# A decode attention kernel: keys and probabilities transposed in 32x32 blocks on VectorE instead of on TensorE, with 128-column block-diagonal queries and 512-column matmuls

## The chip, the cores and the metric

The kernel runs on one core of a Trainium2 chip. Times are device microseconds of that core. "Span" is the time from the first to the last instruction in a profiled execution; the device time is some 1.7 us longer (198.0 and 199.75 us for the profiled run of the kernel before). All runs quoted are in the fast state (within 1.5% of the fastest of the same kernel) but one, which is named where it counts. In what follows, SBUF is the on-chip memory that transfers fill, and PSUM the eight banks into which TensorE writes; VectorE and ScalarE read both.

## The reference, cut to what matters

Four sequences each decode one token. The result is a gate times windowed attention, plus one minus the gate times a small feed-forward network. Attention has 32 query heads on 8 key/value heads of width 128 and looks at the last 4096 positions of the cache.

```python
q = (x @ wq).reshape(B, Sq, Hq, Dh)               # B=4, Sq=1, D=512, Hq=32, Dh=128
k = k_cache[:, :, Sk - W:, :]                     # Hkv=8, W=4096; each serves 4 query heads
v = v_cache[:, :, Sk - W:, :]
p = softmax(einsum("bhqd,bhkd->bhqk", q, k) * Dh ** -0.5)
a = einsum("bhqk,bhkd->bhqd", p, v).reshape(B, Sq, Hq * Dh) @ wo
b = ((relu(x @ W_gate)) * (x @ W_up)) @ W_down
out = g * a + (1 - g) * b                         # g = sigmoid(sum(x * gate_w))
```

All of it is bf16. 81 MB are read from memory, 67 MB of them keys and values, each used once.

## The kernel before

The work is cut into eight **sets**: one sequence and four key/value heads each. A set is 4.19 MB of keys and 4.19 MB of values. Keys arrive with positions on partitions. Scores need the head's width on partitions, so keys must be transposed. Before, TensorE does this, two bf16 at a time as one fp32, and VectorE and ScalarE share the copies out of PSUM:

```python
def KT(s, g):                                     # TensorE: 4 transposes fill one bank, 16 such groups in a set
    for q in range(4):
        c = 4 * g + q
        tp(bk[:, 128 * q:128 * (q + 1)], kf[:, 128 * c:128 * (c + 1)], identf[:, :], ...)

def EKT(s, g):                                    # VectorE (10 of 16) or ScalarE (6 of 16): back over the keys
    E.op(lambda: v.tensor_copy(kt_dst(s, g), bankb[tr(key)]), ev=("E",) + key, waits=[key])

def SC(s, f):                                     # scores: four column groups of 32 side by side, mask last
    for e in range(3):
        for c in range(4):
            lhsT, rhs = (maskl, maskr) if e == 2 else (qblk[:, s, e, :], kt[:, ck:ck + 4, :, e])
            mm(bk[32 * c:32 * c + 32, :], lhsT, rhs, e == 0, e == 2, ..., pos=(0, 32 * c))

def PV(s):                                        # probabilities times values, four side by side
    for c in range(16):
        for q in range(4):
            mm(ob(s)[32 * q:32 * q + 32, :], pT[:, s % 2, c, 32 * q:32 * q + 32],
               slot("v", s)[:, 256 * ck:256 * ck + 256], c == 0, c == 15, ..., pos=(0, 32 * q))
```

Each set then goes: four score blocks (`SC`), each reduced on VectorE (`ESC`); the row maximum over all four, shared between partitions by a small matmul (`MAX`, `SW`, `ESW`), which gives the negated maximum `negmax`; the exponential on ScalarE (`EXP`); the transposes of the probabilities (`PT`, TensorE, with copies `EPT`); the row sums (`RS`); the values (`PV`), normalised (`NORM`) and folded (`OQ`). The values of set s-1 are computed within set s. TensorE's order is fixed in the program:

```python
for s in range(1, NSET):
    o += kt(s, 0) + [("PT", s - 1), ("RS", s - 1)] + kt(s, 1) + [("SC", s, 0)] + kt(s, 2) + [("SC", s, 1)]
    o += kt(s, 3) + [("SC", s, 2), ("PV", s - 1), ("SC", s, 3), ("SW", s), ("OQ", s - 1)]
```

Five 4 MB slots in SBUF take the transfers in turn. A slot is asked for again when its reader is done.

## Time and profile before

| | before |
|---|---|
| time, median of 4 runs | 199.74 us (199.66 to 199.81) |
| span of the profiled run | 198.0 us |
| DMA | in all slices but the first and the last two at 90% or more |
| busiest engine | TensorE, 74% of the span |
| first and last `negmax` ready | 34.0 and 170.6 us, 19.5 us apart on average |

In the page's rows of slices each digit is the busy share, in tenths, of a fortieth of the span. In a timeline, the columns are start, duration, engine, line, operation, output and inputs, count and, in brackets, how long the engine sat idle before and what ended that. Most of the lines themselves are in the prediction below. These two are the first and the last maximum, ready at 34.04 and 170.58 us:

```profile
33.89 0.15 DVE L564 TENSOR_SCALAR negmax<-hmax 128x1 f32<-128x1 f32 x1
...
170.43 0.15 DVE L564 TENSOR_SCALAR negmax<-hmax 128x1 f32<-128x1 f32 x1
```

### The profile page before, as it was taken

To read this page: it belongs to the slowest core of one execution; us is meant where nothing else is said; L and a number is where in the kernel's file an instruction comes from. 1 tells how busy PE (TensorE), PEld (TensorE's weight loads), DVE (VectorE), ACT (ScalarE), POOL (GpSimd) and SP (SyncE) were. 2 spreads that over 40 slices of the span, in tenths; PEclk is the share of its full clock that TensorE was granted. 3 is DMA by queue.
4 is the path that set the end of the run, shared out by engine and by line. 5 is a ranking of instruction groups with operands and counts; after the bars stand their busy time and mean duration, and the time that the engine had idled before them with its cause. 6 is when DMAs were issued, how large, how long until landed. Compare 5 with 4: busy or idle time off the path is not lost.

```text
span 198.0 us, 4187 instructions
## 1 busy us (share of the span) xinstructions
PE 147.5 (74%) x1856; PEld 116.4 (59%) x1856; DVE 105.3 (53%) x245; ACT 67.4 (34%) x70; POOL 13.2 (7%) x38
## 2 busy tenths in 40 slices
PE   0029865999199949982998399929993999297854
PEld 0029732977197729762976397629772978155531
DVE  3005766786358747862786268626863676431100
ACT  2005721453425343434353425342534253410000
POOL 7774000000000000000000000000000000000000
PEclk9999999699859987999699669975998599855589
DMA  5999999999999999999999999999999999999981
GB/s 212 424 425 424 425 427 437 443 447 419 420 437 437 427 430 424 427 437 434 430 437 420 420 419 450 427 425 443 420 430 427 423 407 440 448 399 412 414 333 39
DMA packets 3946, 81.28 MB, mean 410 GB/s; under 512 B 588, under 2 KB 600, under 8 KB 984
## 3 DMA queue, kind: packets, MB, share of 16 engines
q1 hardware_dynamic: 3920, 81.01, 95.9%
q8 instruction: 14, 0.23, 0.5%
q14 instruction: 4, 0.03, 0.0%
q10 hardware_dynamic: 8, 0.00, 0.0%
HBM read 81.01 MB, written 0.00 MB: 409 GB/s over the span
## 4 chain that ended last, share of the span: by engine, by line
DMA 65%; PE 23%; SPq 7%; DVE 3%; issue 1%
DMA slots<-in_A_k_cache_dram 49%; DMA slots<-in_A_wo_dram 17%; PE bank L331 16%; SPq L258 7%; PE bank L327 7%; DVE qblk L542 1%; DVE sc L552 0%; DVE pe L527 0%; DVE slots L520 0%; DVE osum L600 0%; DVE pe L529 0%; DVE xT L523 0%
## 5 line engine op out<-in xcount | busy, mean ns | idle before, releaser
L331 PE MATMUL bank<-identf,slots 128*128 128x128 f32 x512 | 75.5, 311 | 28.5 <-DMA slots<-in_A_k_cache_dram 28.5
L331 PEld LDWEIGHTS bank<-identf,slots 128*128 128x128 f32 x512 | 68.3, 164 | 35.7 <-DMA slots<-in_A_k_cache_dram 29.2
L520 DVE COPY slots<-bank 128x1024 bf16<-128x1024 bf16 x80 | 54.4, 690 | 50.6 <-PE bank L331 49.4
L613 ACT ACTIVATE slots<-bank 128x1024 bf16<-128x1024 bf16 x48 | 47.6, 1022 | 65.2 <-PE bank L331 65.2
L635 ACT ACTIVATE pe<-sc,negmax 128x2048 bf16<-128x2048 bf16 x8 | 16.0, 2001 | 37.8 <-DVE negmax L564 37.8
L552 DVE TENSOR_SCALAR_CACHE_REDUCE sc<-bank 128x512 bf16<-128x512 f32 x32 | 22.1, 692 | 3.5 <-PE bank L327 1.2
L327 PE MATMUL bank<-slots,qblk 128*32 128x512 bf16 x256 | 20.3, 392 | 1.4 <-DVE qblk L542 1.2
L327 PE MATMUL bank<-slots,pT 128*32 128x256 bf16 x512 | 17.0, 291 | 0.7 <-DMA slots<-in_A_v_cache_dram 0.7
L327 PEld LDWEIGHTS bank<-slots,pT 128*32 128x32 bf16 x512 | 14.2, 103 | 3.5 <-DMA slots<-in_A_v_cache_dram 0.8
L331 PE MATMUL bank<-identb,pe 128*128 128x128 bf16 x128 | 13.7, 291 | 2.2 <-ACT pe L635 2.2
L331 PEld LDWEIGHTS bank<-identb,pe 128*128 128x128 bf16 x128 | 12.9, 139 | 2.7 <-ACT pe L635 2.3
L570 DVE COPY pT<-bank 128x1024 bf16<-128x1024 bf16 x16 | 10.9, 690 | 4.6 <-PE bank L331 4.5
L327 PE MATMUL bank<-maskr,maskl 128*32 128x512 bf16 x128 | 12.5, 377 | 0.0
L578 DVE TENSOR_SCALAR osb<-bank,recip 128x256 bf16<-128x256 f32 x8 | 3.9, 484 | 12.0 <-PE bank L327 12.0
L327 PEld LDWEIGHTS bank<-rd,grpb 128*128 128x128 bf16 x8 | 0.8, 96 | 14.2 <-DVE rd L558 14.2
L327 PE MATMUL bank<-rd,grpb 128*128 128x8 bf16 x8 | 1.4, 180 | 10.1 <-DVE rd L558 10.1
L327 PEld LDWEIGHTS bank<-slots,qblk 128*32 128x32 bf16 x256 | 4.6, 95 | 6.2 <-issue 3.5
L327 PE MATMUL bank<-slots,oq 128*4 128x256 bf16 x64 | 4.5, 272 | 2.6 <-DMA slots<-in_A_wo_dram 1.9
L327 PEld LDWEIGHTS bank<-maskr,maskl 128*32 128x32 bf16 x128 | 3.3, 94 | 3.9
L327 PEld LDWEIGHTS bank<-slots,oq 128*4 128x4 bf16 x64 | 2.3, 83 | 5.0 <-DMA slots<-in_A_wo_dram 3.4
L327 PE MATMUL bank<-slots,xT 128*4 128x512 bf16 (+1 forms) x64 | 5.1, 476 | 0.0
L327 PE MATMUL bank<-osb,fold 128*64 128x32 bf16 x64 | 3.6, 189 | 0.7 <-DVE osb L578 0.7
(57 smaller groups left out, 57.7 us busy)
## 6 DMA issues: line engine op xcount, KB each, us to landing
slots<-in_A_k_cache_dram SPq DMA_DIRECT2D x8, 4096.0 KB, 42.5
slots<-in_A_v_cache_dram SPq DMA_DIRECT2D x8, 4096.0 KB, 33.7
slots<-in_A_wq_dram SPq DMA_DIRECT2D x1, 4096.0 KB, 21.2
slots<-in_A_wo_dram SPq DMA_DIRECT2D x3, 1024.0 KB, 39.6
slots<-in_B_W_gate_dram SPq DMA_DIRECT2D x1, 1792.0 KB, 37.5
slots<-in_B_W_up_dram SPq DMA_DIRECT2D x1, 1792.0 KB, 40.8
wdsb<-in_B_W_down_dram SPq DMA_DIRECT2D x1, 1792.0 KB, 35.4
slots<-in_A_wo_dram SPq DMA_DIRECT2D x1, 512.0 KB, 42.4
```

The source lines that it names most:

```text
L258: E.op(lambda: e.dma_start(dst, src), ev=ev, waits=waits, ctr=ctr)
L327: E.op(lambda: t.matmul(out_, lhsT, rhs, start=start, stop=stop, tile_position=pos, skip_group_check=True), ev=ev, waits=waits)
L331: E.op(lambda: t.transpose(out_, in_, idn), ev=ev, waits=waits)
L520: E.op(lambda: v.tensor_copy(kt_dst(s, g), bankb[tr(key)]), ev=("E",) + key, waits=[key])
L542: E.op(lambda dst=dst, r=r, b=b: v.tensor_copy(dst, src[r, :, :, :, b]), ev=("E",) + key if (u, b) == (1, 3) else None, waits=[key, ("QZ",)])
L552: E.op(lambda: v.tensor_scalar(sc[:, 512 * f:512 * f + 512], banks[scb(key)], 1.0, None, op0=ALU.mult, op1=ALU.max, accum_out=mx4[:, f:f + ...
L570: E.op(lambda: v.tensor_copy(dst, bankb[tr(key)]), ev=("E",) + key, waits=[key] + ([("PV", s - 2)] if s >= 2 else []))
L578: E.op(lambda: v.tensor_scalar(osb[:, s % 2, :], ob(s), recip[:, s % 2:s % 2 + 1], None, op0=ALU.mult), ev=("NORM", s), waits=[("E", "RS", ...
L613: E.op(lambda: a.activation(kt_dst(s, g), bankb[tr(key)], ACTF.Copy), ev=("E",) + key, waits=[key])
L635: E.op(lambda: a.activation(pe[:, :], sc[:, :], ACTF.Exp, bias=negmax[:, s % 2:s % 2 + 1], scale=SCALE, accum_out=rowsum[:, s % 2:s % 2 + ...
```

## The change

The intent is to take the transposes off TensorE and to do without the PSUM round trip. VectorE can transpose 32x32 blocks from SBUF to SBUF. Four instructions transpose a set's keys, one its probabilities. As the blocks stay in their place on the partitions, the queries are laid out as block diagonals of 128 columns, so that matmuls over the whole array pick the right rows. The diff is cut to what matters; `...` marks what is left out.

```diff
-NSLOT = 5
+NSLOT = 4
...
+    sb("kt", [128, 4, 4096], BF16)               # transposed keys, one set; later the down-projection weights
-    sb("qblk", [128, NSET, 2, 32], BF16)
+    sb("qblk", [128, NSET, 4, 144], BF16)
...
     for s in range(1, NSET):
-        o += kt(s, 0) + [("PT", s - 1), ("RS", s - 1)] + kt(s, 1) + [("SC", s, 0)] + kt(s, 2) + [("SC", s, 1)]
-        o += kt(s, 3) + [("SC", s, 2), ("PV", s - 1), ("SC", s, 3), ("SW", s), ("OQ", s - 1)]
+        o += [("KT", s, 0), ("PT", s - 1), ("KT", s, 1), ("SC", s, 0), ("KT", s, 2), ("SC", s, 1), ("KT", s, 3), ("SC", s, 2)]
+        o += [("RS", s - 1), ("PV", s - 1), ("SC", s, 3), ("SW", s), ("OQ", s - 1)]
...
-        frees[n] = {"k": [("SC", it[-1], 3)], ...
+        frees[n] = {"k": [("E", "KT", it[-1], 3)], ...
...
+        def EKT(s, f):                            # VectorE
+            w = [("K", s)] + ([("SC", s - 1, f)] if s else [])
+            E.op(lambda: v.transpose(kt[:, f, :].bitcast(FP32), slot("k", s)[:, 4096 * f:4096 * f + 4096].bitcast(FP32)),
+                 ev=("E", "KT", s, f), waits=w)
+        def EPT(s):
+            E.op(lambda: v.transpose(pT[:, s % 2, :], pe[:, :]), ev=("E", "PT", s),
+                 waits=[("EXP", s)] + ([("PV", s - 2)] if s >= 2 else []))
...
+        def SC(s, f):                             # TensorE: 8 + 1 matmuls, 128 x 512 each
+            for t in range(2):
+                for h in range(2):
+                    for e in range(2):
+                        mm(bk, qblk[:, s, 2 * h + e, 16 - 16 * t:144 - 16 * t], kv[:, t, :, h, :, e], ...)
+            mm(bk, R["maskl"][:, :], R["maskr"][:, :], False, True, ev=key)
+        def PV(s):                                # 32 matmuls of 512 columns, two side by side
+            for f in range(4):
+                for c in range(0, 16, 2):
+                    mm(ob(s)[r:r + 64, :], pT[:, s % 2, x:x + 64], vv[:, f, :, c:c + 2, :], ..., pos=(0, r))
```

"KT" and "PT" in the order now stand for VectorE's instructions alone. Also part of the change: `NORM` and the fold's eviction move from VectorE to ScalarE; the queries' block diagonals take 64 small copies (half on VectorE, half on ScalarE) for 16; the down-projection weights wait for the last scores, because they share memory with `kt`; the PSUM banks are dealt out anew (three for scores for two, two for values for one, two for transposes for four); and a 64-byte load at the end of the DMA queue goes.

## The prediction

> **What bounds the kernel now.** I read the busy page first (the slices, then the chain that ended last), then the waits, and last the timeline of one set in the middle.
>
> ```profile
> span 198.0 us, 4187 instructions
> PE 147.5 (74%) x1856; PEld 116.4 (59%) x1856; DVE 105.3 (53%) x245; ACT 67.4 (34%) x70; POOL 13.2 (7%) x38
> ...
> DMA  5999999999999999999999999999999999999981
> ...
> HBM read 81.01 MB, written 0.00 MB: 409 GB/s over the span
> ...
> DMA 65%; PE 23%; SPq 7%; DVE 3%; issue 1%
> ```
>
> The reader is to see that the DMA row is at 9 in all slices but the first and the last, and that no engine comes near that. The slices move some 429 GB/s. The kernel is bound by reading 81.01 MB; about 10 us beyond 81.01/0.429 = 189 us are start and end. One set (one batch, four key/value heads) reads 2 x 4.19 MB = 8.39 MB, so **a set arrives every 19.6 us**. The waits say the same from the engines' side:
>
> ```profile
> PEld bank L331 <- DMA slots<-in_A_k_cache_dram: 29.2, 8, 13.4
> PE bank L331 <- DMA slots<-in_A_k_cache_dram: 28.5, 8, 13.4
> ```
>
> TensorE waits for each of eight key tiles: computing is ahead of the data. The timeline of set 6 shows by how much, and has the durations that I need:
>
> ```profile
> 133.01 3.68 PE L331 MATMUL bank<-identf,slots 128*128 128x128 f32 x16 [2.83 <-DMA slots<-in_A_k_cache_dram]
> ...
> 146.24 1.91 PE L327 MATMUL bank<-slots,pT 128*32 128x256 bf16 x64
> ...
> 148.89 0.69 DVE L552 TENSOR_SCALAR_CACHE_REDUCE sc<-bank 128x512 bf16<-128x512 f32 x1
> ...
> 150.52 0.15 DVE L564 TENSOR_SCALAR negmax<-hmax 128x1 f32<-128x1 f32 x1
> ...
> 150.71 2.00 ACT L635 ACTIVATE pe<-sc,negmax 128x2048 bf16<-128x2048 bf16 x1 [4.42 <-DVE negmax L564]
> ```
>
> Keys land at 133.0; the negated maximum, which closes a set's scores and releases its exponential, is there at 150.67. So a set needs 17.7 us from keys to maximum, and 2 us are left before the next keys. That slack is what the change may use up. From the last score block's matmuls being done (148.89) to the maximum is 1.8 us. The first maximum is there at 34.04, the last (set 7) at 170.58, seven periods of 19.5 us, the pace of the DMA.
>
> **What the Trainium skill says.** (1) "VectorE: DVE Perf Modes", the three transpose paths: VectorE transposes only 32x32 blocks, 128x128 bf16 in 311 ns. Less its fixed cost of some 150 cycles this is one element per cycle at 0.96 GHz. (2) "Vector Engine (DVE) Microarchitecture Reference", section 3.8: the transpose array sustains "one element per cycle per lane". The trace before has no such instruction, so no number agrees or disagrees; its PSUM copy (1024 bf16, 690 ns = 512/0.96 + 157) does agree with the fixed cost. (3) "TensorE: Matmul & The Clock Gate", back-to-back issue gap: N/2.4 + 2.5 ns, 216 ns for 512 columns. It agrees: from the start of the probability matmuls above to the next group on TensorE (146.24 to 147.99) are 1.75 us, for 16 rounds of four 256-column matmuls side by side 109 ns each (the formula gives 109). (4) The same page, Part 1: after an idle window of 3.4 us the clock is halved. [...]
>
> **The change part by part**, per set.
> Removed from TensorE: 64 fp32 key transposes and 16 of the probabilities (75.5 + 13.7 us in the groups, 11 us a set). Removed from VectorE and ScalarE: the copies that emptied them (54.4 + 47.6 + 10.9 us, 14 us a set).
> Added to VectorE: four transposes of 128x2048 fp32 for keys, one of 128x2048 bf16 for probabilities. Estimate from (1) and (2): (2048 + 150)/0.96 = **2.3 us each, 11.5 us a set**. With four score reductions (4 x 0.70), the maximum (0.16 + 0.23, 0.17 + 0.15, 0.3 of waiting in between) and a reciprocal (0.16), VectorE has 15.5 us a set: below 19.6.
> TensorE's matmuls get longer: scores are 4 x 9 matmuls of 512 full-array columns (before 3 rounds of four side by side per block), 9 x 0.22 = 2.0 us a block against 0.65. Probabilities times values: 32 matmuls of 512 columns, two side by side, 16 x 0.216 = 3.5 us against 1.75. TensorE sums to some 12.5 us a set, also below 19.6.
>
> Neither engine is full. But **they take turns**. With 0 at set s-1's maximum, VectorE does: key block 0 to 2.35; probabilities of s-1 (ScalarE's exponential ends at 2.2, hidden) to 4.65; block 1 to 6.95; score reduction 0 to 7.7; block 2 to 10.0; reduction 1 to 10.75; block 3 to 13.05; reduction 2 to 13.8. TensorE's score block 2 can start at 10.0 and ends at 12.2; then, in program order, come the row sum (0.3) and the probabilities times values (3.5), to 16.0, and only then score block 3, 2.0 plus some 0.15 of pipeline, to 18.1. VectorE, idle since 14, takes 1.8 more to the maximum. **Period 19.9 us** at full clock. With 0.85 in score block 2, values and score block 3 it is 21.3. TensorE idles over 4 us from a set's end to the next first score block, so it goes cold; but a cold block 0 ends before its reduction starts. I take **20.2 us**.
>
> Start: k0 lands at 13.3 as before, x and its transpose by 14.3, four key transposes to 23.6. Wq is there at some 23.2 (arrival pace); queries cold, copied by VectorE (0.69 + 3 x 0.29) to 26.8; eight fp32 transposes; block-diagonal copies: 64 small ones in place of 16, half on VectorE (0.13 each), half on ScalarE behind them (0.18 each), to some 36. Scores of set 0: 36.3 + 4 x 2.0 + 2 for cold start and pipeline, maximum 1.8: **first maximum at 47, against 34.0** before. Keys of set 1 land at 34.3, so this is on the path now.
>
> End, from the last maximum N: exponential 2.2, row sum and the gate/up matmuls (3.2, as measured) to 5.9, product and its transpose to 7.7, values 4.5 (partly cold) to 12.2, normalise and fold 1.6, down projection 3.15, its eviction 0.5, output projection 4.2, combine and store 2.3: **N + 23**. The down-projection weights now share memory with the transposed keys and wait for the last scores (N - 1.9); with 1.8 + 4.2 MB behind that they land by N + 14, before the output projection needs the last. Hidden.
>
> Sum: 47 + 7 x 20.2 + 23 = **211 us**.
>
> Four slots for five: keys s+2 are asked for when set s's last key block is transposed, 13 us into the set; the queue holds three further transfers (29 us) when k_s lands. With computing 13 us behind the data at set 1 the queue just stays fed; later it may run dry for a little, which costs nothing while computing sets the pace.
>
> **Rivals.**
> (a) Data still bounds: 198 to 200. For it: both engines' sums (15.5, 12.5) are under 19.6. It needs a period under about 18.3, as 47 + 7 x 18.3 + 23 = 198; for this a transpose must take under 1.9 us. Against: the turn-taking above.
> (b) The fp32 transpose takes two cycles an element (4.4 us): then VectorE has 24 us a set, and the total passes 235. Against: (2) makes no difference between types; the trace can't tell.
> (c) Slot starvation by four slots makes it slower even with a fast VectorE. Against: the queue count above; it could add 2 to 5 us only.
>
> **Range and chances.** Period +-0.8 us counts seven times (+-6), start +-2, end +-2: 203 to 219 for 8 in 10. Faster by 2% (under 195.8) would need fewer bytes than 81 MB: 2%. Within 2% (under 203.8) needs rival (a) or a period of 19.1: 14%. Slower: 84%.
>
> **What would show each step right or wrong.** A key transpose of 2.3 us (wrong below 1.9 or above 2.8). Maxima 20 us apart, the first at 47. DMA slices below 9 late in the span, with no key-tile wait of TensorE left; VectorE's longest wait before the fourth score reduction, for TensorE, some 4 us each. The chain that ended last through VectorE and TensorE rather than the DMA. If maxima are 19.5 apart and the DMA row stays at 9, I am wrong through rival (a); if VectorE is at 95% in mid-span, through (b).

## The result and the profile after

The changed kernel takes 208.06 us (median of 4 runs, 206.22 to 209.0) against 199.74 us: a ratio of 1.0405, with a 95% interval of 1.0324 to 1.0487. Ratios here are the mean time of one kernel's fast runs over that of the other's of the same rounds, so not quite the ratio of the medians. It is slower by 4%, inside the predicted range and 3 us below the predicted 211.

The page of the profiled run (209.0 us, the slowest of the four) has these lines where those of before were shown:

```profile
span 207.3 us, 2287 instructions
...
PE 136.1 (66%) x936; PEld 60.8 (29%) x936; DVE 127.0 (61%) x193; ACT 31.3 (15%) x72; POOL 14.0 (7%) x38
...
DMA  5999999999977999999999999999999999849950
...
HBM read 81.01 MB, written 0.00 MB: 391 GB/s over the span
...
PE 46%; DVE 37%; DMA 10%; issue 3%; ACT 2%; SPq 1%; DVEq 0%; ACTq 0%
```

TensorE has 11 us less to do and ScalarE 36 us less. Still the span is 9 us longer. The DMA's row has holes at slices 11 and 12 (counted from 0), 34 and 35, and near the end. The first hole is a slot that comes free late (the keys of set 3 are asked for at 62.11 us, when set 1's are transposed); the second is the down-projection weights, which are asked for at 183.50, after the last scores. The chain that ended last was 65% DMA and is 10% DMA; TensorE and VectorE make up 83% of it, though neither is busy for more than 66%.

The groups of instructions give the new durations (busy us, mean ns, then the idle time in front of them):

```profile
L506 DVE STREAM_TRANSPOSE kt<-slots 128x2048 f32<-128x2048 f32 x32 | 73.2, 2294 | 0.0
L534 DVE TENSOR_SCALAR_CACHE_REDUCE sc<-bank 128x512 bf16<-128x512 f32 x32 | 21.4, 668 | 41.6 <-PE bank L314 41.6
...
L550 DVE STREAM_TRANSPOSE pT<-pe 128x2048 bf16<-128x2048 bf16 x8 | 18.5, 2312 | 2.2 <-ACT pe L612 2.2
```

A key transpose takes 2.29 us, as estimated, and never waits for keys: the data is always there. The longest part of VectorE's idle time, 41.6 us of some 80, is ahead of the score reductions, for TensorE. The timeline of a set in the middle shows which:

```profile
108.02 2.30 DVE L506 STREAM_TRANSPOSE kt<-slots 128x2048 f32<-128x2048 f32 x1
...
117.64 1.91 PE L314 MATMUL bank<-kt,qblk 128*128 128x512 bf16 x8 [0.68 <-DVE kt L506]
...
119.81 3.64 PE L314 MATMUL bank<-slots,pT 128*64 128x512 bf16 x32
...
120.91 0.16 DVE L555 RECIPROCAL recip<-bank 128x1 f32<-128x1 f32 x1
...
123.39 1.91 PE L314 MATMUL bank<-kt,qblk 128*128 128x512 bf16 x8
...
125.56 0.69 DVE L534 TENSOR_SCALAR_CACHE_REDUCE sc<-bank 128x512 bf16<-128x512 f32 x1 [4.49 <-PE bank L314]
...
127.26 0.15 DVE L546 TENSOR_SCALAR negmax<-hmax 128x1 f32<-128x1 f32 x1
```

From 108.02 VectorE transposes and reduces without a stop. TensorE starts score block 2 at 117.64, as soon as its keys are transposed. Then it computes the values of the set before (119.81), 3.6 us, and only at 123.39 score block 3. VectorE is done with all else at 121.07 and waits 4.49 us. The next `negmax` is ready at 127.41, 19.31 us after the last (108.10).

Where did the time go? Three numbers add up to the span: the first `negmax` is ready at 48.70 us (34.04 before), the last at 185.37, seven periods of 19.5 us later, and 21.9 us follow (27.4 before).

```profile
48.55 0.15 DVE L546 TENSOR_SCALAR negmax<-hmax 128x1 f32<-128x1 f32 x1
...
185.22 0.15 DVE L546 TENSOR_SCALAR negmax<-hmax 128x1 f32<-128x1 f32 x1
```

Against the kernel before, the start is 14.7 us longer, the seven periods together 0.1 us, and the end is 5.5 us shorter: 9.3 us in all. So the periods are no longer than they were. What is lost is lost at the start, and the question is why the later sets do not win it back.

### The profile page after: what moved, and what is told of

Read it like the earlier page. It is cut to its first block, busy times and chain, and to the rows that moved or that the text cites. A ratio compares the mean times of both kernels' runs of the same rounds, so it can differ in the third digit from the quotient of the medians.

```text
span 207.3 us, 2287 instructions
## 1 busy us (share of the span) xinstructions
PE 136.1 (66%) x936; PEld 60.8 (29%) x936; DVE 127.0 (61%) x193; ACT 31.3 (15%) x72; POOL 14.0 (7%) x38
## 4 chain that ended last, share of the span: by engine, by line
PE 46%; DVE 37%; DMA 10%; issue 3%; ACT 2%; SPq 1%; DVEq 0%; ACTq 0%
PE bank L314 45%; DVE kt L506 20%; DMA slots<-in_A_wq_dram 10%; DVE pT L550 8%; DVE sc L534 4%; DVE qblk L493 2%; ACT pe L612 1%; PE bank L318 1%; ACT qblk L587 1%; DVE rd L540 1%; SPq L247 1%; DVE hmax L545 1%; DVE negmax L546 1%; DVE rowmax L538 1%; ACT osb L590 0%
## 5 line engine op out<-in xcount | busy, mean ns | idle before, releaser
L314 PE MATMUL bank<-kt,qblk 128*128 128x512 bf16 x256 | 75.8, 446 | 27.0 <-DVE kt L506 24.9
L506 DVE STREAM_TRANSPOSE kt<-slots 128x2048 f32<-128x2048 f32 x32 | 73.2, 2294 | 0.0
L534 DVE TENSOR_SCALAR_CACHE_REDUCE sc<-bank 128x512 bf16<-128x512 f32 x32 | 21.4, 668 | 41.6 <-PE bank L314 41.6
L314 PEld LDWEIGHTS bank<-kt,qblk 128*128 128x128 bf16 x256 | 25.4, 108 | 72.5 <-DVE kt L506 33.5
L314 PE MATMUL bank<-slots,pT 128*64 128x512 bf16 x256 | 30.4, 393 | 0.0
L590 ACT ACTIVATE osb<-bank,recip 128x512 bf16<-128x512 f32 x8 | 5.5, 687 | 101.6 <-PE bank L314 101.6
L550 DVE STREAM_TRANSPOSE pT<-pe 128x2048 bf16<-128x2048 bf16 x8 | 18.5, 2312 | 2.2 <-ACT pe L612 2.2
L314 PEld LDWEIGHTS bank<-slots,pT 128*64 128x64 bf16 x256 | 14.3, 113 | 12.4 <-issue 1.5
L314 PE MATMUL bank<-maskr,maskl 128*128 128x512 bf16 x32 | 13.6, 424 | 0.0
L318 PE MATMUL bank<-identb,xsb 4*128 4x4 bf16 x4 | 0.3, 173 | 13.4 <-DMA xsb<-in_A_x_dram 13.4
L314 PE MATMUL bank<-rd,grpb 128*128 128x8 bf16 x8 | 1.3, 168 | 10.9 <-DVE rd L540 9.3
L314 PEld LDWEIGHTS bank<-osb,fold 128*64 128x64 bf16 x128 | 4.6, 112 | 1.5 <-ACT osb L590 1.3
L314 PEld LDWEIGHTS bank<-rd,grpb 128*128 128x128 bf16 x8 | 0.8, 95 | 14.7 <-issue 12.9
L493 DVE COPY qblk<-bank 32x32 bf16<-32x32 bf16 x32 | 4.0, 179 | 0.9 <-PE bank L318 0.8
L318 PEld LDWEIGHTS bank<-identb,xsb 4*128 4x128 bf16 x4 | 0.2, 115 | 13.4 <-DMA xsb<-in_A_x_dram 13.4
```

Of the source, the lines that this page charges most:

```text
L314: E.op(lambda: t.matmul(out_, lhsT, rhs, start=start, stop=stop, tile_position=pos, skip_group_check=True), ev=ev, waits=waits)
L318: E.op(lambda: t.transpose(out_, in_, idn), ev=ev, waits=waits)
L493: E.op(lambda dst=dst, r=r, g=g, e=e, src=src: copy(dst, src[r, g, 0:B, e, :, :]), ev=("E",) + key if (q, g, e) == (3, 1, 1) else None, wa ...
L506: E.op(lambda: v.transpose(kt[:, f, :].bitcast(FP32), slot("k", s)[:, 4096 * f:4096 * f + 4096].bitcast(FP32)), ev=("E", "KT", s, f), waits=w)
L534: E.op(lambda: v.tensor_scalar(sc[:, 512 * f:512 * f + 512], banks[scb(key)], 1.0, None, op0=ALU.mult, op1=ALU.max, accum_out=mx4[:, f:f + ...
L550: E.op(lambda: v.transpose(pT[:, s % 2, :], pe[:, :]), ev=("E", "PT", s), waits=[("EXP", s)] + ([("PV", s - 2)] if s >= 2 else []))
```

## The experiments

**Theory.** No engine is full, and none waits for keys or values: the only waits for the DMA are for `x`, the gate's and the query weights, at the start. VectorE and TensorE take turns in each set, and the values stand between score blocks 2 and 3 on TensorE, so the period is a sum of both engines' work (19.3 us). That is about the pace of the DMA (19.6 us a set), but the first set's maximum is nearly 15 us later than before. The data is there, and a shorter period could use it to catch up; this one can't.

**Rivals.** Four slots starve the DMA. Or VectorE's own work, 14.4 us in each period, is the bound in some way. Or the cold clock of TensorE stretches the period.

All experiments were one change, or two together where it is said, to the changed kernel, except where the kernel before is named. Each was compared with runs of the kernel before on the same chip.

### Values moved behind the last score block

```diff
-        o += [("RS", s - 1), ("PV", s - 1), ("SC", s, 3), ("SW", s), ("OQ", s - 1)]
+        o += [("SC", s, 3), ("RS", s - 1), ("SW", s), ("PV", s - 1), ("OQ", s - 1)]
```

> The changed kernel with one thing moved on TensorE: the probabilities times values of set s-1 come after the fourth score block and the maximum of set s, not between its third and fourth score block. Turn-taking theory: the 4.5 us that VectorE waits before its fourth score reduction shrink to about 1.6 us, the compute period falls from 19.3 to about 16.4 us, so from some set on the DMA (19.6 us a set) sets the pace again; first maximum stays at 48.7; time 201 to 204 us. Rival, VectorE's own work is the bound: nothing moves, 206 to 209. Rival, starved slots: maxima stay 19.3 apart with holes in the DMA row, 206 to 209.

Measured: 199.11 us (198.41 to 201.08, 20 runs), ratio 0.9989 (0.9968 to 1.0009). The same instructions, in another order, take back all of the 4%. The timeline of a set in the middle:

```profile
109.65 1.91 PE L314 MATMUL bank<-kt,qblk 128*128 128x512 bf16 x8 [0.68 <-DVE kt L506]
...
111.81 0.69 DVE L534 TENSOR_SCALAR_CACHE_REDUCE sc<-bank 128x512 bf16<-128x512 f32 x1 [1.63 <-PE bank L314]
...
113.21 3.64 PE L314 MATMUL bank<-slots,pT 128*64 128x512 bf16 x32
...
113.71 2.00 ACT L612 ACTIVATE pe<-sc,negmax 128x2048 bf16<-128x2048 bf16 x1 [11.68 <-DVE negmax L546]
...
130.34 2.00 ACT L612 ACTIVATE pe<-sc,negmax 128x2048 bf16<-128x2048 bf16 x1 [11.68 <-DVE negmax L546]
```

VectorE's wait is 1.63 us for 4.49, and the exponentials, each released by `negmax`, are 16.63 us apart. The values now run while VectorE transposes the next set. The last two periods of this run are 18.2 and 20.6 us: the DMA paces again. The page shows one shallow hole left in its row:

```profile
DMA  5999999999998999999999999999999999999991
```

The expected period (16.4) and wait were right; the time was below the expected 201 to 204. The hole cost only some 1 us (346 GB/s in slice 12, of 4.9 us, where 430 is usual). VectorE did the same work (127.5 us busy), so its work was not the bound. The four slots were the same too.

### Values moved forward, behind the first score block

```diff
-        o += [("KT", s, 0), ("PT", s - 1), ("KT", s, 1), ("SC", s, 0), ("KT", s, 2), ("SC", s, 1), ("KT", s, 3), ("SC", s, 2)]
-        o += [("RS", s - 1), ("PV", s - 1), ("SC", s, 3), ("SW", s), ("OQ", s - 1)]
+        o += [("KT", s, 0), ("PT", s - 1), ("KT", s, 1), ("SC", s, 0), ("RS", s - 1), ("PV", s - 1), ("KT", s, 2), ("SC", s, 1)]
+        o += [("KT", s, 3), ("SC", s, 2), ("SC", s, 3), ("SW", s), ("OQ", s - 1)]
```

> The same matmuls (row sums, probabilities times values of set s-1) moved the other way, to right after the first score block of set s, where TensorE is idle. Turn-taking: they delay the second score block by about 1 us, compute period about 17.5 us, then the DMA paces; time 201 to 204 us. VectorE's own work or starved slots: 206 to 209.

Measured: 202.16 us (201.93 to 203.52), ratio 1.0151 (1.0116 to 1.0186). The time is as expected, but six of the seven periods were 18.4 to 18.9 us (one was 17.3), not 17.5. The timeline and the table by stretches show why. A line of the table has the stretch and its length, the busy us of PE (TensorE), PEld (its weight loads), DVE (VectorE), ACT (ScalarE) and POOL, then the granted clock, the DMA share and the GB/s:

```profile
126.19 4.38 PE L314 MATMUL bank<-slots,pT 128*64 128x512 bf16 x32
...
132.66 0.69 DVE L534 TENSOR_SCALAR_CACHE_REDUCE sc<-bank 128x512 bf16<-128x512 f32 x1 [2.27 <-PE bank L314]
```

```profile
124.00:128.00 4.00, 4.00 (x18) 2.00 (x18) 4.00 (x3) 0.00 (x0) 0.00 (x0) 0.57 0.93 401
128.00:131.00 3.00, 3.00 (x27) 1.40 (x24) 2.39 (x4) 0.33 (x1) 0.00 (x0) 1.00 1.04 442
```

TensorE had been nearly idle before, its clock was at 0.57, and the cold stretch now held the end of the first score block and the start of the values, which took 4.38 us for 3.64. Score block 1 came late by that, and VectorE waits 2.27 us for it.

### The same with TensorE kept warm

Nine matmuls of no use, into an idle bank, in each set's idle time:

```diff
+        def WARM(s):
+            for i in range(9):
+                mm(banks[ACC], identb[:, :], R["maskr"][:, :], True, True, waits=[("GE",), ("IDB",), ("MR",)])
...
-        ... ("SW", s), ("OQ", s - 1)]
+        ... ("SW", s), ("OQ", s - 1), ("WARM", s)]
```

> e1b (values right after the first score block) with the same nine filling matmuls. e1b had a period of 18.8 where 17.5 was expected, with the values at clock 0.57. If the cold clock is what was missing: period 17.5 us or less (then the DMA's 19.6 sets the pace later on), values in 3.6 instead of 4.4 us, time 199.5 to 201.5. If it is something else: stays 18.8 and 202.

Measured: 199.65 us (198.48 to 200.64, 20 runs), ratio 0.9999 (0.9982 to 1.0016), from 1.0151. The timeline shows the values at 3.64 us again, and the first exponentials of the run 17.2 to 17.3 us apart (47.65, 64.85, 82.13, 99.40), until transfers pace it:

```profile
104.80 3.64 PE L314 MATMUL bank<-slots,pT 128*64 128x512 bf16 x32 [0.92 <-DMA slots<-in_A_v_cache_dram]
```

So the cold clock was the missing 1.5 us a set (18.8 to 17.3), and here matmuls that compute nothing save 2.5 us.

### The changed kernel, in its own order, kept warm

The same nine matmuls in the changed kernel:

> The changed kernel with nine matmuls of no use (512 columns, into an idle bank, 1.9 us at full clock) put on TensorE into its idle time after each set's maximum, so that its clock should not fall. If the cold clock costs nothing because only the first score block runs cold and VectorE does not need it yet: the later periods stay 19.3, only the first two (20.0) shorten; 205 to 207.5 us and less spread. If the cold clock is a part of the period: 19.3 falls by over 0.5 us and the time below 204.

Measured: 207.55 us (205.67 to 209.05, four runs). The slowest counts as a slow run, being 1.6% above the fastest; the three fast ones are 205.67, 206.68 and 208.42. Their ratio is 1.0359 (1.0307 to 1.041): within the interval of the changed kernel, with the same spread of 2.8 us. In part the expectation failed. The exponentials of this run lie 19.2, 19.3, 20.1, 20.1, 20.2, 19.3 and 19.3 us apart. The first score block is warm now, but in three sets the clock fell after it, and the second score block ran cold:

```profile
107.64 1.91 PE L314 MATMUL bank<-kt,qblk 128*128 128x512 bf16 x8
...
112.08 2.73 PE L314 MATMUL bank<-kt,qblk 128*128 128x512 bf16 x8 [2.32 <-DVE kt L510]
...
115.27 0.69 DVE L538 TENSOR_SCALAR_CACHE_REDUCE sc<-bank 128x512 bf16<-128x512 f32 x1 [0.43 <-PE bank L314]
```

VectorE does wait for that one, and the set takes 0.8 us more. So it counts where the cold stretch falls: on score block 0 it is hidden (periods of 19.31 us in the changed kernel), on score block 1 it costs some 0.8 us (here, and in the changed kernel's first two periods, 19.95 and 20.13 us). Whether the spread of 206 to 209 us comes from this alone is open: one profile for each kernel can't tell, and filling did not narrow it.

### Query weights before the first keys

```diff
-    o = [("k", 0), ("x",), ("gw",), ("wq",), ("k", 1), ("v", 0)]
+    o = [("x",), ("gw",), ("wq",), ("k", 0), ("k", 1), ("v", 0)]
...
-    o = [("XT",), ("Z",), ("KT", 0, 0), ("KT", 0, 1), ("KT", 0, 2), ("KT", 0, 3), ("Q",), ("QT",)]
+    o = [("XT",), ("Z",), ("Q",), ("QT",), ("KT", 0, 0), ("KT", 0, 1), ("KT", 0, 2), ("KT", 0, 3)]
```

> The changed kernel with only the start changed: query weights are loaded before the first keys, and query projection, transposes and block-diagonal copies go before the four key transposes. Theory that the start counts in full once computing sets the pace: first maximum at about 38 instead of 48.7 us; the period stays 19.3; the kernel comes near the DMA's bound, 198.5 to 201.5 us. Rival, the start is hidden behind transfers as in the kernel before: 206 to 209.

Measured: 200.18 us (199.97 to 201.56), ratio 1.007 (1.0034 to 1.0105). The first exponential starts at 40.49 us for 48.74, 2.5 us later than expected, and the DMA's row is full but for its last slices. The periods stay 19.2 to 20.2 us. So an earlier start alone takes back 3.4 of the 4.05%: at a period near the DMA's pace, what is lost at the start stays lost.

### Both, values early

> e1b and e2 together. If turn-taking and the late start are the whole of the loss, the DMA row is full again and the time is the DMA's: 198.5 to 200.5 us, the same as the kernel before within 1%. If something else of the change costs (four slots, shared memory for the down-projection weights, contention of VectorE's transposes with the transfers), it stays over 202 us.

Measured: 199.88 us (198.55 to 201.35, 12 runs), ratio 1.0008 (0.9979 to 1.0037), the same as the kernel before. The two repairs do not add up. Alone they took back 2.5 and 3.4 points of the 4.05, together 4.0, all that there was: a shorter period catches up with the late start, and an early start leaves little to catch up with. Nothing else in the change costs time that shows.

### Both, values last

> Values last (as in e1) and query first (as in e2) together. e1 had a compute period of 16.6 us and one hole in its DMA row at 60 us (1 us lost); query first should close it by bringing the first maximum from 47.5 to some 40 us. Theory: the DMA row is full, the compute period leaves it 3 us a set, time 197 to 199 us, some 1% under the kernel before. If the transfers' rate is all, it is equal to e1: 199.

Measured: 198.46 us (198.26 to 198.6, 6 runs), ratio 0.9936 (0.9915 to 0.9957). This is the best version, 0.6% under the kernel before. In its page the DMA's row has no hole:

```profile
DMA  6999999999999999999999999999999999999991
```

The exponentials are 16.3, 16.6 and 17.3 us apart in the first sets, and 18.9 to 20.2 us in the last four periods, the pace of the data. Its span is 196.5 us for 198.0. Its last weights are used from 193.78 us, before from 195.27, though the same bytes are read; why they land earlier is not settled.

### The kernel before with four slots

```diff
-NSLOT = 5
+NSLOT = 4
```

> The kernel before with four slots for five and nothing else. Theory (my rival c is of no weight): the slots are asked back early enough, 199 to 200.5 us. If four slots starve the DMA by themselves: over 202 us, with holes in the DMA row.

Measured: 199.65 us (199.21 to 199.86, 12 runs), ratio 0.9993 (0.9981 to 1.0006). The fifth slot was worth nothing; starvation by the slot count alone is out. The first hole in the changed kernel's DMA row comes from a slot that is released late, because computing is late, and the second from the down-projection weights' wait for the last scores.

### The kernel before without the small last load

> The kernel before without the small load at the end of its queue, which the change also removed. Theory: of no weight, 199 to 200.5 us, ratio to the kernel before within 0.3%. If it hastens the last weights' landing: up to 1 us slower.

Measured: 199.77 us (199.39 to 200.47, 14 runs), ratio 1.0001 (0.9988 to 1.0013). Of no weight.

### Half of the values

```diff
-            for f in range(4):
+            for f in range(2):                    # and stop at (1, 12), (1, 14)
```

> Wrong result on purpose: the changed kernel with half of the matmuls of probabilities times values (16 for 32 in a set). VectorE's work is untouched. Turn-taking: they stand between score blocks 2 and 3 in full, so the period falls by 16 x 0.108 = 1.75 us to 17.6 us, VectorE's wait before its fourth reduction from 4.5 to 2.75; 200.5 to 203 us. If VectorE's work is the bound: 19.3 stays, 206 to 209.

Measured: 199.23 us (198.55 to 200.89, 20 runs), ratio 0.9985 (0.9968 to 1.0001); the result is wrong, as intended. The time is below the expected 200.5 to 203. The exponentials in the middle are 17.59 us apart, where 17.6 was worked out, and the timeline has the wait:

```profile
81.20 0.69 DVE L534 TENSOR_SCALAR_CACHE_REDUCE sc<-bank 128x512 bf16<-128x512 f32 x1 [2.77 <-PE bank L314]
...
83.09 2.00 ACT L612 ACTIVATE pe<-sc,negmax 128x2048 bf16<-128x2048 bf16 x1 [3.21 <-DVE negmax L546]
```

The values that were cut were on the path in full: 1.72 us taken away (3.64 to 1.92), 1.72 us gained in each period.

### Half of each key transpose

```diff
-            E.op(lambda: v.transpose(kt[:, f, :].bitcast(FP32), slot("k", s)[:, 4096 * f:4096 * f + 4096].bitcast(FP32)),
+            w2 = 2048 if s else 4096
+            E.op(lambda: v.transpose(kt[:, f, 0:w2].bitcast(FP32), slot("k", s)[:, 4096 * f:4096 * f + w2].bitcast(FP32)),
```

> Wrong result on purpose: the changed kernel, each key transpose after set 0 over half the columns (1024 fp32). Sizes the transposes' share of the period. Turn-taking: block 0 ends at 1.15, but the probabilities' transpose then waits for the exponential (2.15), so that of three transposes on the path only 2.3 us fall out, not 3.3: period 17.0 us, then paced by the DMA; 200.5 to 203 us. If VectorE's work were the bound: 19.3 less 4 x 1.1, 14.9 us. If TensorE or the DMA were: 19.3 stays.

Measured: 199.16 us (197.87 to 200.58, 20 runs), ratio 0.9969 (0.9949 to 0.999), below the expected 200.5 to 203. The comparison with the reference still calls the result correct, although half of the keys of sets 1 to 7 are those of set 0: it does not see this error. VectorE has 28 us less to do (98.9 us), 4.0 us in each of seven sets; a period falls by 1.9 us (17.40 for 19.31 in the five later sets), not by those 4.0, and the probabilities' transpose waits for the exponential:

```profile
105.31 2.31 DVE L551 STREAM_TRANSPOSE pT<-pe 128x2048 bf16<-128x2048 bf16 x1 [1.01 <-ACT pe L613]
...
118.68 0.69 DVE L535 TENSOR_SCALAR_CACHE_REDUCE sc<-bank 128x512 bf16<-128x512 f32 x1 [4.98 <-PE bank L314]
```

I had expected 17.0. In its place the path goes over to TensorE earlier: score block 2 follows block 1 without a gap, and VectorE waits 0.47 us before reduction 1 and 4.98 us before reduction 3.

## Why the prediction was right, point by point

- **The bound and the slack.** That the kernel before was bound by the DMA holds: variants with quite different computing (values last, half of the values, half of the key transposes) all end at 199 us too. The 2 us of slack a set are TensorE's waits for keys in the trace before (28.5 us in eight, 13.4 of them at the start). A small misreading: the DMA row is below 9 in the last two slices, not only in the last.
- **Transposes on VectorE.** 2.3 us each was estimated from the Trainium skill's one element per cycle ("Vector Engine (DVE) Microarchitecture Reference", section 3.8). Measured: 2.29 us for fp32 and 2.31 us for bf16. Rival (b), two cycles for fp32, is out.
- **Taking turns.** The step that carried the prediction, that VectorE idles from 14 to 18 us into the set while TensorE computes values and score block 3, is there: 4.49 us, from 13.0 to 17.5 us into the set. Moving the values (period 16.63 us) and halving them (17.59 us) show it.
- **The period, mis-sized.** "I take **20.2 us**": it was 19.31, and 20.0 in the first two sets. Two terms were off. Transposes in a row start 2.25 us apart, not 2.3 (108.02 and 110.27 are such starts), and the reductions were shorter, 0.59 us up to the next instruction's start, for 0.70; so the third key block was transposed 9.5 us into the set, for 10.0. And the allowance for a clock of 0.85 was needed in the first two sets only, where score block 1 ran cold (0.6 to 0.8 us each). The five later ones are 19.31 to 19.33 us; for one of them, the table by stretches of the changed kernel puts the cold clock on score block 0, and full clock on all that VectorE waits for:

```profile
110.30:114.70 4.40, 3.53 (x9) 1.10 (x9) 4.40 (x4) 0.06 (x1) 0.00 (x0) 0.66 0.92 391
114.70:117.60 2.90, 2.13 (x9) 0.78 (x9) 2.90 (x5) 0.00 (x0) 0.00 (x0) 1.00 1.13 486
117.60:126.90 9.30, 7.92 (x53) 3.73 (x53) 4.55 (x10) 0.69 (x1) 0.00 (x0) 1.00 0.95 412
```

- **What the sum says of the cause.** Against the kernel before, the prediction put 13 us on the start, 4.9 on the periods and -4.4 on the end; measured are 14.7, 0.1 and -5.5. The share of the periods was not there. Maxima 19.5 us apart were even the sign named for rival (a), but with the DMA row at 9, and that row has holes, no transpose waits for keys, and VectorE waits 4.49 us for TensorE. That the period of turn-taking (19.3) falls on the DMA's pace (19.6) is chance, as far as the runs show.
- **The start.** 47 us predicted, 48.70 measured. The queries were ready at 35.6 us (36 predicted); the four score blocks took 10.9 us for 10, and the maximum 2.1 us for 1.8. The printed 47 is not the sum of its own terms (36.3 + 8 + 2 + 1.8 = 48.1): a slip of 1.1 us.
- **The end.** 23 us predicted (its terms add up to 24), 21.9 measured: up to the fold the terms hold within 0.3 us, but the down projection took 1.7 us, not 3.15, as the granted clock was 1.00 there (0.50 before), and the output projection 3.7 us, not 4.2. The shared memory was hidden, as said: the down-projection weights were asked for at 183.5, took 7.0 us, and were used from 198.9. But the DMA stood nearly still for them, at 164 and 16 GB/s from 180 to 184 us.
- **The sum.** It gave a span and was put down as a time. The 1.7 us between the two were forgotten, and hid part of the 4.7 us that the seven periods were too long. That the errors cancel in part is luck. The errors are start -1.7, periods +4.7, end +1.1, span for time -1.7: 2.4 us in all, between the summands' 211.4 and the profiled run's 209.0.
- **Rival (a)**, data still bounds, needed a period of 18.3. With values last (16.6 us), or values early and TensorE kept warm (17.3 us), the kernel reaches it, and there the time is 198 to 200 us, as that rival said.
- **Rival (c)**, slots, is out as a cause of the 4%. But the queue, which the prediction had "just" fed at set 1, ran dry there (279 and 147 GB/s from 60 to 64 us).
- **The clock.** Point (4) of the prediction also called it an agreement that the clock was 0.66 in 73 to 78 us; the sentence is cut, as the idle time there was 1.5 us and not 3.4.

## What to carry to other kernels

Before work is moved from one engine to another, add up the dependent chain of one period over both engines, and not only each engine's share: here neither is busy for more than 66%, and the sum of their turns sets the pace. Work of an earlier period that nobody waits for, like the values here, belongs behind the instruction that another engine does wait for; that reordering alone was worth 4%. If the period is close to the pace of the transfers, a late first period is never made up, so load first what the longest chain needs.

## What the Trainium skill lacked or had wrong

- "VectorE: DVE Perf Modes", The three transpose paths, has one duration, for 128x128 bf16, and nothing for fp32. Here 128x2048 took 2.29 us in fp32 and 2.31 us in bf16, and 128x1024 fp32 took 1.20 to 1.24 us: 1024 elements more take some 1.07 us more, 0.96 a ns. The rate of one element per cycle at 0.96 GHz holds for fp32 as for bf16, so a pair of bf16 that is moved as one fp32 costs half.
- "TensorE: Matmul & The Clock Gate", Why this matters for your kernels (the table), warns of idle gaps of over some 3 us. Here shorter gaps did it: 2.06 us (score block 0 at clock 0.66, with only small matmuls and 1.3 us of idle time before it), and 2.32 us behind 4.2 us of matmuls without a stop (2.73 us for 1.91), this one in three sets and not in the other sets with the same gap. It also lacks that a cold stretch is free where nobody waits for its matmuls, and that filling matmuls can move it to a worse place: 20.1 for 19.3 us a set.
- "DMA: Bandwidth & Descriptors", Where 436 GB/s comes from, says that some 358 GB/s of memory bandwidth bind transfers from memory to SBUF. One core alone read at 399 to 450 GB/s in all slices of the kernel before but the first and the last two, 409 GB/s over its span. The 425 GB/s that the page itself has measured agree. Its sentence on what binds does not hold for a core that reads alone, and leaves out what the page says above it, under its table: that this is a single core's number, and some 358 GB/s each core's part when both read. No run here has two cores.
